# A chunked attention and feed-forward kernel on one core: another order for loads, copies and matmuls

## The chip, the cores and the metric

The kernel runs on one core of one Trainium2 chip. The core has TensorE (PE) for matrix products, VectorE (DVE), ScalarE (ACT) and GpSimd (POOL) for element-wise work, and SyncE (SP), which here only issues transfers. Each engine has a program of its own, and runs it in order. Transfers (DMA) run on 16 DMA engines; here POOL issues the loads (the software queue, q0), and SP the stores and the transpositions from SBUF to SBUF (the hardware queue, q1). The metric is the device time of one execution in microseconds (us); the median of several runs counts.

## What is computed

For 4 batches of 768 tokens and 8 heads of 64, each chunk of 32 queries attends to 8 memory keys and to the keys from 16 before to 8 after the chunk. The result, with heads side by side as rows of 512, goes through a layer norm and a two-layer network, and is added to itself:

```python
for c in range(nc):                      # chunk 32, left 16, right 8
    ...
    k_full = np.concatenate([mem_k, k_ctx], axis=2)
    v_full = np.concatenate([mem_v, v_ctx], axis=2)
    scores = scale * np.matmul(q_c, k_full.transpose(0, 1, 3, 2))
    scores = scores - np.max(scores, axis=-1, keepdims=True)
    a = np.exp(scores)
    a = a / (np.sum(a, axis=-1, keepdims=True) + 1e-09)
    out[:, :, c_start:c_end] = np.matmul(a, v_full)
...
xn = (x - mu) / np.sqrt(var + 1e-06) * g_ln
ch = np.maximum(xn @ w_ch1, 0.0) @ w_ch2      # 512 -> 2048 -> 512
return (x + ch).astype(np.float32)
```

## The kernel before

**Tiles and turns.** 128 tokens are a token tile; a batch has six (t = 0 to 5), the program 24. Three token tiles make a turn u of the network, so there are eight turns (0 to 7), and batch b fills turns 2b and 2b + 1. A turn has U = 28 steps. Steps 0 to 15 are up steps (`up`, line 331: xT times a piece of W1, then a ReLU into rT on ACT or DVE by turns), steps 16 to 27 are down steps (`down`, line 357: rT times W2); after the last one of a tile, `finish` (line 366, DVE) makes the output tile osb and SP stores it. Turn 0 has most of its up steps in the front, the hand-written stretch before the turns; there and in turn 1 some are tile-wise (`up_tile`, line 342: one token tile, four pieces).

**Attention of a token tile.** `scores` (line 244, PE) needs the keys KT and the queries QR of the tile; `soften` (line 254, ACT) takes the exponential; `values` (line 265, PE) needs V, and on DVE it divides and sums (lines 272 to 279); `norm` (line 285, DVE) makes xn; `turn_x` transposes xn into xT, in turns 0 and 1 with PE (line 313) and a copy, later with a DMA transposition on SP (line 308). `stats` (line 290, ACT) and `root` (lines 296 and 300, POOL) give rstd for `finish`. `attend(i, s0, s1, u)` puts these at steps s0 (scores), s0 + 1, s1 (values), s1 + 1 (norm) and s1 + 2 (turn_x, stats) of turn u.

**How K, Q and V come in.** In batch 0 `load_tile` loads K and Q by token tile, and `turn_tile` transposes them with PE (line 194) and copies them to KT and QR. In batches 1 to 3 `load_pair` loads a block of 256 tokens (blk 0, 1, 2), K and Q in two pieces of 128 KB each (line 125); `mix` copies a block into iv with its halves interleaved (line 102, the copy helper); `cross` transposes iv on SP (line 221) into rawk (keys) or QR (queries); `spread` copies rawk to the places in KT where chunks and their neighbours need it (DVE and ACT, lines 102 and 100). `load_v` loads one of twelve V pieces (88 KB, line 133), `v_mem` copies the memory values into V, `mem_cols` the memory keys into KT. There are two sets of KT, QR and V, two rawk, four iv, and eight load buffers st.

**What sets the order.** Nothing is scheduled by a tool: the program is written by hand, and every engine gets its instructions in the order in which the Python emits them. `at(u, step, ...)` puts a call behind the matmuls of a step; `ahead` spreads a list of calls over steps. Where two calls have one step, the one put down first comes first. So a step's number says behind which others a call stands in the queue of its engine, and not when it runs. The loads on POOL wait as well for the one issued eight before.

For batch b > 0 the list `order` (line 596) holds loads, `mem_cols`, `v_mem` and `mix`, all on POOL. Batch 1's list begins at step 23 of turn 0; batches 2 and 3 have theirs in turns 2 and 4. Transpositions and spreads stand in a table of (block, step): for batch 1 `cross` at 27 of turn 0 and at 1 and 14 of turn 1, each spread four steps after that number; for the others `cross` at 7, 12 and 24 and the spread four steps later.

## Time and profile before

| | before |
|---|---|
| median of 3 runs | 265.72 us (264.95 to 266.97) |
| the profiled execution | 263.43 us, its span 261.7 us |
| PE busy | 220.0 us (84%) |
| POOL, DVE, ACT busy | 142.7, 122.3, 97.6 us |
| mean granted clock of PE | 0.908 |
| HBM | 29.82 MB read, 6.29 MB written |

A span reaches from the first to the last instruction of the profiled execution; times in the rows count from its start. In brackets behind a row stands how long the engine had been idle just before, and whose end released it. The lines are those of the kernel before. In this execution turn 0's first down step begins at 43.23 us, turn 1 at 59.58, turn 2 at 103.23, turn 3 at 136.63, turn 4 at 163.21 and turn 5 at 189.29.

### The profile page before, as it was taken

What the parts mean: (1) busy time and instruction counts of PE and PEld (TensorE: products, weight loads), DVE (VectorE), ACT (ScalarE), POOL (GpSimd) and SP (SyncE); (2) the same over time, 40 slices, a digit from 0 to 9 for tenths busy, and PEclk for the clock granted to TensorE, in tenths of its full rate; (3) what the DMA queues carried; (4) which work ended last, traced back from release to release, by engine and by line L of the source; (5) the groups of instructions that cost most, each with busy time, mean ns of one, the idle gap of its engine ahead of it and who ended that gap; (6) DMA issues with size and microseconds to landing.
All of it is one profiled execution on the core that took longest, in us unless ns stands there. A gap on an engine that the chain in (4) does not pass through costs nothing.

```text
span 261.7 us, 5110 instructions
## 1 busy us (share of the span) xinstructions
PE 220.0 (84%) x2048; PEld 132.2 (51%) x2048; DVE 122.3 (47%) x288; ACT 97.6 (37%) x195; POOL 142.7 (55%) x188
## 2 busy tenths in 40 slices
PE   7545988988074998999419999999799999999994
PEld 2324874446053844664105654664366456546653
DVE  5534266475033555570533652582557436443312
ACT  2321255443034461690203740492267216512300
POOL 8936279999817978993494268998301201110000
PEclk9955599999656899999956999999999999999999
DMA  5999999998999998999999937999943230122012
GB/s 78 150 183 196 202 181 130 126 107 131 116 92 129 118 142 133 158 79 90 97 187 98 143 49 124 149 123 129 192 98 23 66 97 10 34 60 80 3 40 80
DMA packets 105448, 28.93 MB, mean 111 GB/s; under 512 B 93392, under 2 KB 101840, under 8 KB 105424
## 3 DMA queue, kind: packets, MB, share of 16 engines
q0 software_dynamic: 72320, 14.84, 65.9%
...
HBM read 29.82 MB, written 6.29 MB: 138 GB/s over the span
## 4 chain that ended last, share of the span: by engine, by line
PE 47%; DMA 26%; POOL 18%; issue 4%; DVE 2%; ACT 2%; POOLq 0%; ACTq 0%; DVEq 0%
DMA st<-in_q_dram 22%; PE mm L331 19%; PE mm L357 18%; POOL V L133 7%; POOL st L125 4%; DMA rawk<-iv 3%; PE mm L342 3%; POOL iv L102 3%; PE att L244 2%; PE att L265 2%; POOL rstd L300 1%; PE mm L379 1%; DMA xT<-xn 1%; POOL V L102 1%; POOL st L117 1%
## 5 line engine op out<-in xcount | busy, mean ns | idle before, releaser
L331 PE MATMUL mm<-xT,w1c 128*128 128x384 f16 (+1 forms) x480 | 86.3, 333 | 12.7 <-DMA xT<-xn 11.7
L357 PE MATMUL mm<-w2c,rT 128*128 128x512 f16 x368 | 83.8, 379 | 0.0
L331 PEld LDWEIGHTS <-w1c 128*128 128x128 f16 x480 | 53.1, 117 | 36.8 <-DMA xT<-xn 10.8
L325 DVE TENSOR_SCALAR rT<-mm 128x384 f16<-128x384 f32 (+2 forms) x65 | 35.6, 549 | 40.7 <-PE mm L331 33.2
L357 PEld LDWEIGHTS <-rT 128*128 128x128 f16 x368 | 34.6, 98 | 38.8
L323 ACT ACTIVATE rT<-mm 128x384 f16<-128x384 f32 (+2 forms) x65 | 31.2, 483 | 59.9 <-PE mm L331 28.1
L133 POOL DMA_DIRECT2D V<-in_v_dram x48 | 44.3, 929 | 1.9 <-DMA st<-in_k_dram 1.0
L296 POOL TENSOR_SCALAR veps<-sq 128x1 f32<-128x1 f32 x24 | 5.9, 248 | 57.0 <-ACT junk L290 34.9
L254 ACT ACTIVATE AT<-att,band 96x512 f16<-96x512 f32 x48 | 31.2, 678 | 7.4 <-PE att L244 7.3
L100 ACT COPY KT<-rawk 128x288 f16<-128x288 f16 (+1 forms) x18 | 12.2, 726 | 45.6 <-DMA rawk<-iv 45.6
L366 DVE SCALAR_TENSOR_TENSOR osb<-mm,rstd,xs 128x512 f32<-128x512 f32 x23 | 17.1, 749 | 24.3 <-PE mm L357 18.6
L102 POOL COPY iv<-st 128x1024 f16<-128x1024 f16 x18 | 19.0, 1074 | 16.4 <-DMA st<-in_q_dram 8.5
L290 ACT ACTIVATE junk<-xs,nmean 128x512 f16<-128x512 f32 x24 | 17.2, 716 | 15.0 <-DVE nmean L279 10.9
L102 DVE COPY KT<-rawk 128x704 f16<-128x704 f16 x9 | 8.4, 936 | 30.6 <-DMA rawk<-iv 30.6
L102 POOL COPY V<-memv 8x2560 f16<-8x2560 f16 x9 | 21.3, 2362 | 0.0
L342 PE MATMUL mm<-xT,w1c 128*128 128x128 f16 x160 | 14.2, 263 | 7.6 <-ACT rT L323 3.8
L285 DVE SCALAR_TENSOR_TENSOR xn<-xs,nmean,gb 128x512 f16<-128x512 f32 x24 | 19.9, 829 | 0.4
L342 PEld LDWEIGHTS <-w1c 128*128 128x128 f16 x160 | 13.4, 129 | 8.4 <-issue 8.0
L273 DVE SCALAR_TENSOR_TENSOR xs<-att,rec 128x512 f32<-128x512 f32 x24 | 16.6, 692 | 0.8
L300 POOL TENSOR_TENSOR rstd<-veps,mhalf 128x1 f32<-128x1 f32 x24 | 13.9, 579 | 2.0
L244 PEld LDWEIGHTS <-KT 64*96 64x96 f16 x384 | 11.4, 129 | 6.8 <-issue 4.5
L244 PE MATMUL att<-QR,KT 64*96 64x64 f16 x384 | 14.2, 216 | 0.6 <-DVE KT L102 0.6
...
## 6 DMA issues: line engine op xcount, KB each, us to landing
...
st<-in_k_dram POOLq DMA_DIRECT2D x24, 128.0 KB, 8.2
st<-in_q_dram POOLq DMA_DIRECT2D x24, 128.0 KB, 9.6
...
```

Source lines behind the costliest of these rows:

```text
L102: eng.tensor_copy(out=out, in_=in_)
L133: nc.gpsimd.dma_start(out=V[b % 2][lo:hi, g, :, 0:64], in_=dram(v, b * H * HS + (64 * g - 24 + lo) * D, [[64, hi - lo], [HS, H], [1, 64]]),)
L244: nc.tensor.matmul(out=p[0:W, par, (4 * gg + j) * 64 : (4 * gg + j) * 64 + 64], lhsT=KT[b % 2][rows, 2 * t + gg, j, :], rhs=free(QR[b % 2] ...
L254: nc.scalar.activation(out=free(AT[t % 3], 32 * c, [[64, 16], [1, 32]]), in_=free(p, 4 * c, [[64, 16], [1, 4], [8, 8]], W), func=ACTF.Exp, ...
L285: nc.vector.scalar_tensor_tensor(out=xn[i % 4], in0=xs[i % 9], scalar=nmean[t], in1=gb, op0=ALU.add, op1=ALU.mult,)
L290: nc.scalar.activation(out=junk, in_=xs[(NT * b + t) % 9], func=ACTF.Square, bias=nmean[t], scale=1.0, accum_out=sq[t],)
L323: nc.scalar.activation(out=o, in_=p, func=ACTF.Relu)
L325: nc.vector.tensor_scalar(out=o, in0=p, scalar1=0.0, scalar2=None, op0=ALU.max)
L331: nc.tensor.matmul(out=p, lhsT=free(w1c[c][:, dt, :], i, [[4, 128]]), rhs=xT[u % 2][:, dt, 128 * lo : 128 * (lo + n)], start=(dt == 0), st ...
L342: nc.tensor.matmul(out=p[:, 128 * k_ : 128 * k_ + 128], lhsT=free(w1c[c][:, dt, :], k_, [[4, 128]]), rhs=xT[u % 2][:, dt, 128 * i : 128 * ...
L357: nc.tensor.matmul(out=p, lhsT=rT[c][:, k_, 128 * i : 128 * i + 128], rhs=w2c[c][:, k_, :], start=(c == 0 and k_ == 0), stop=(c == 3 and k ...
L366: nc.vector.scalar_tensor_tensor(out=o, in0=p, scalar=rstd[t % 9], in1=xs[t % 9], op0=ALU.mult, op1=ALU.add,)
```

## The change

The computation stays as it is. What moves:

- **Front, loads.** The layer-norm weights gb are loaded first of all, from ACT's queue instead of SP's and without the memset ahead. On POOL V pieces 0 and 1 come ahead of query tile 1, and W1 chunk 1 ahead of query tile 2 and key tile 3.
- **Front, PE.** Values and norm of tile 0, its up steps, and tile 1 up to its first up steps come ahead of the transposition of query tile 2 and of key tile 3. W1 chunk 2's up steps move from turn 0 into the front, tile-wise: turn 0 keeps steps 12 to 15. One small key copy goes to ACT. The casts of the memory values of batches 1 to 3 move from the front into turn 0's steps 22 to 24, and batch 1's buffers are cleared at step 15 instead of 12.
- **Batch 1.** The first two blocks are interleaved by ACT (keys) and DVE (queries) at steps 5 and 9 of turn 1, and by POOL only the third; POOL's list keeps the loads and `mem_cols`, and starts at step 21 of turn 0. Transpositions stand at steps 6, 10 and 19, spreads at 12, 15 and 27, scores of tiles 0 to 2 at 13, 16 and 19. `v_mem` goes to DVE.
- **Batches 2 and 3.** Each call has its own step: loads at 0 to 2 and 13, V at 1, 9, 14 to 17 and 21 to 24, `mix` (POOL) at 8, 12 and 20, `cross` at 14, 18 and 26, spreads at 20, 24 and at 4 of the next turn; `v_mem` on DVE at 21, 23, 25.

```diff
-                copy(e0, free(kt, 768 * t - 384 + 88, [[96, 4], [1, 8]]),
+                copy(eo or e0, free(kt, 768 * t - 384 + 88, [[96, 4], [1, 8]]),
...
+    nc.scalar.dma_start(out=gb, in_=dram(moe_g_ln, 0, [[0, 128], [1, 512]]))
     nc.sync.dma_start(out=memkf, in_=dram(mem_k, 0, [[64, 128], [128 * 64, 2], [1, 64]]))
...
-    load_tile(0, 1, 1)
     load_v(0, 0)
     load_v(0, 1)
+    load_tile(0, 1, 1)
     load_tile(0, 2, 0)
     load_w1(0)
     load_v(0, 2)
     load_v(0, 3)
+    load_w1(1)
     load_tile(0, 2, 1)
     load_tile(0, 3, 0)
-    load_w1(1)
...
-    turn_tile(0, 2, 0, dve, act, mm[0])
+    values(0, 0)
+    norm(0, 0)
+    turn_tile(0, 2, 0, dve, act, mm[0], act)
     warm(1)
     scores(0, 1)
     soften(0, 1, 0)
     soften(0, 1, 1)
-    values(0, 0)
-    norm(0, 0)
-    warm(2)
-    turn_tile(0, 2, 1, dve, act, mm[2])
     turn_x(0, 0)
     warm(2)
+    up_tile(0, 0, 0, act)
     values(0, 1)
     norm(0, 1)
+    warm(3)
+    turn_x(0, 1)
+    warm(1)
+    up_tile(0, 0, 1, dve)
+    up_tile(0, 1, 0, act)
+    turn_tile(0, 2, 1, dve, act, mm[2])
     turn_tile(0, 3, 0, dve, act, mm[1])
-    up_tile(0, 0, 0, act)
     scores(0, 2)
...
-    at(0, 9, v_mem, 0, 6, NG, dve)
-    at(0, 12, early, 1)
+    at(0, 14, v_mem, 0, 6, NG, dve)
+    at(0, 15, early, 1)
+    for b in range(1, B):
+        at(0, 14, load_mem_v, b)
+        at(0, 21 + b, mem_vals, b)
...
+            order = [(load_pair, (0,)), (load_pair, (1,)), (mem_cols, (pool,))]
+            order += [(load_v, (g,)) for g in range(6)] + [(load_pair, (2,))]
+            order += [(load_v, (g,)) for g in range(6, 12)]
+            ahead(1, order, 21, 0.25)
+            at(1, 5, mix_pair, 1, 0, act, dve)
+            at(1, 6, cross_pair, 1, 0)
+            at(1, 9, mix_pair, 1, 1, act, dve)
+            at(1, 10, cross_pair, 1, 1)
+            at(1, 12, spread, 1, 0, dve, act)
+            at(1, 15, spread, 1, 1, dve, act)
...
-            ahead(b, order, U * (u - 1), 1)
...
+            at(w, 14, cross_pair, b, 0)
+            at(w, 18, cross_pair, b, 1)
+            at(w, 26, cross_pair, b, 2)
+            at(w, 20, spread, b, 0, dve, act)
+            at(w, 24, spread, b, 1, dve, act)
...
-                    if step >= 8:
+                    if step >= 12:
```

How the instructions stand now, at three places. A minus marks a row of the kernel before, a plus one of the kernel after, and a row without either stands in both; instructions that only wait are not shown.

POOL, the loads of batch 1: V_96 is batch 1's V, iv the interleaved blocks, st the load buffers, memv the memory values, memKT the memory keys.

```order
 L102 COPY KT_98<-memKT 128x48x8
-L102 COPY V_96<-memv_67 8x2560
-L102 COPY iv_89<-st_87 128x2x8x64
-L102 COPY iv_90<-st_88 128x2x8x64
 L133 DMA V_96<-in_v_dram 72x8x64
-L133 DMA V_96<-in_v_dram 88x8x64 x2
-L102 COPY iv_91<-st_81 128x2x8x64
-L102 COPY iv_92<-st_82 128x2x8x64
-L102 COPY V_96<-memv_67 8x2560
-L133 DMA V_96<-in_v_dram 88x8x64 x3
+L133 DMA V_96<-in_v_dram 88x8x64 x5
 L125 DMA st_83<-in_k_dram 128x1x512 x2
```

The copies that stood between the loads are gone from POOL here; behind the first V piece five more follow at once, then the third block.

DVE, turn 1 around the norm of token tile 5 (xn_114<-xs_109): KT_98<-rawk_93 is the spread of batch 1's first block, iv_90<-st_88 the interleaving of its queries, rT a ReLU.

```order
 L273 SCALAR_TENSOR_TENSOR xs_109,tot_131<-att_160,rec_158 128x512
 L279 TENSOR_SCALAR nmean_137<-tot_131 128x1
-L102 COPY KT_98<-rawk_93 128x8x88
-L325 TENSOR_SCALAR rT_120<-mm_161 128x256
+L102 COPY iv_90<-st_88 128x2x8x64
+L325 TENSOR_SCALAR rT_120<-mm_164 128x256
 L285 SCALAR_TENSOR_TENSOR xn_114<-xs_109,nmean_137,gb 128x512
 L318 COPY xT_118<-att_159 128x4x128
```

In the place of the spread, ahead of the norm, stands now a copy that reads loaded data; the spread itself has moved eight rows further back.

SP, turn 2: xT1 is the input of turn 3, one row per token tile, with the last one from xn3_116; the rows into rawk and QR0 are the first two blocks of batch 2.

```order
+L308 DMA_TRANSPOSE xT1_118<-xn1_114 128x4x128
+L308 DMA_TRANSPOSE xT1_118<-xn2_115 128x4x128
 L221 DMA_TRANSPOSE rawk1_94<-iv2_91 128x8x128
 L221 DMA_TRANSPOSE QR0_99<-iv3_92 128x8x128
-L308 DMA_TRANSPOSE xT1_118<-xn1_114 128x4x128
 L221 DMA_TRANSPOSE rawk0_93<-iv0_89 128x8x128
 L221 DMA_TRANSPOSE QR0_99<-iv1_90 128x8x128
-L308 DMA_TRANSPOSE xT1_118<-xn2_115 128x4x128
 L369 DMA out_0_dram<-osb0_123 128x512
 L308 DMA_TRANSPOSE xT1_118<-xn3_116 128x4x128
```

The first two tiles of xT1 now come ahead of all four block transpositions, and the third tile comes directly behind the four and a store.

## Rows read from the trace of the kernel before

**Rows 1.** Busy us by turn: PE, PEld, DVE, ACT, POOL; clock; DMA share; GB/s

```profile
43.23:59.58 16.35, 15.65 (x203) 7.42 (x201) 9.52 (x21) 7.03 (x14) 15.93 (x18) 1.00 0.97 105
59.58:103.23 43.65, 29.98 (x309) 20.77 (x308) 17.95 (x42) 15.47 (x32) 32.88 (x44) 0.80 1.43 126
103.23:127.40 24.17, 24.17 (x208) 13.66 (x208) 9.37 (x21) 10.10 (x21) 16.64 (x16) 1.00 1.51 101
127.40:136.63 9.23, 0.05 (x2) 0.01 (x1) 5.42 (x11) 2.16 (x4) 8.20 (x14) 0.74 1.77 155
136.63:163.21 26.58, 26.48 (x209) 14.65 (x210) 12.03 (x28) 10.87 (x22) 14.69 (x20) 0.90 1.03 107
163.21:187.40 24.19, 24.19 (x209) 13.62 (x207) 14.24 (x30) 12.27 (x24) 21.21 (x24) 1.00 1.54 142
187.40:189.29 1.89, 0.00 (x1) 0.03 (x2) 0.75 (x1) 0.00 (x0) 0.00 (x0) 1.00 1.16 217
```

**Rows 2.** Timeline of PE: start, us, instruction, idle before and its releaser

```profile
19.85 0.63 PE L194 MATMUL mm<-identity,st 64*64 64x64 f16 x16 [3.52 <-DMA st<-in_q_dram]
...
25.45 1.86 PE L342 MATMUL mm<-xT,w1c 128*128 128x128 f16 x16 [2.43 <-ACT KT L100]
...
61.02 1.94 PE L331 MATMUL mm<-xT,w1c 128*128 128x256 f16 x16
...
73.57 0.61 PE L313 MATMUL att<-identity,xn 128*128 128x128 f16 x4 [9.24 <-DVE xn L285]
...
82.26 1.86 PE L342 MATMUL mm<-xT,w1c 128*128 128x128 f16 x16 [3.75 <-ACT rT L323]
...
136.63 4.03 PE L331 MATMUL mm<-xT,w1c 128*128 128x384 f16 x12 [9.18 <-DMA xT<-xn]
```

**Rows 3.** Timeline of DVE, with one row of ACT

```profile
8.38 1.00 DVE L102 COPY V<-memv 8x2560 f16<-8x2560 f16 x1
...
71.72 1.36 ACT L100 COPY KT<-rawk 128x288 f16<-128x288 f16 x2 [8.34 <-DMA rawk<-iv]
71.72 0.81 DVE L102 COPY KT<-rawk 128x704 f16<-128x704 f16 x1 [7.22 <-DMA rawk<-iv]
...
72.77 0.75 DVE L285 SCALAR_TENSOR_TENSOR xn<-xs,nmean,gb 128x512 f16<-128x512 f32 x1
...
127.37 0.81 DVE L102 COPY KT<-rawk 128x704 f16<-128x704 f16 x1 [10.25 <-DMA rawk<-iv]
```

**Rows 4.** Timeline of POOL

```profile
42.58 1.50 POOL L125 DMA_DIRECT2D st<-in_k_dram  x2
...
74.51 1.04 POOL L102 COPY iv<-st 128x1024 f16<-128x1024 f16 x1 [3.53 <-DMA st<-in_k_dram]
79.32 1.04 POOL L102 COPY iv<-st 128x1024 f16<-128x1024 f16 x1 [3.77 <-DMA st<-in_q_dram]
...
85.52 1.44 POOL L125 DMA_DIRECT2D st<-in_k_dram  x2
```

**Rows 5.** Timeline of SP's queue

```profile
61.06 2.84 SPq L221 DMA_TRANSPOSE rawk<-iv  x1
...
131.63 1.24 SPq L308 DMA_TRANSPOSE xT<-xn  x1
```

**Rows 6.** DMA queues (packets, MB, share) in windows 50:53, 72:76, 80:84, 128:132, 188:192

```profile
q0 software_dynamic: 1916, 0.50, 126.1%
...
q1 hardware_dynamic: 773, 0.19, 83.5%
...
q1 hardware_dynamic: 1580, 0.40, 91.9%
...
q0 software_dynamic: 3102, 0.29, 155.3%
...
q1 hardware_dynamic: 2361, 0.92, 102.4%
```

**Rows 7.** Loads of K: transfers, KB each, median us from issue to landing

```profile
st<-in_k_dram POOLq DMA_DIRECT2D x24, 128.0 KB, 8.2
```

More of the change, by code (lines that the diff above doesn't have):

```diff
@@ L395, in warm, with load_mem_v @@
             nc.tensor.matmul(out=p[:, 0:m], lhsT=zero[:, 0:128], rhs=zero[:, 0:m], start=True, stop=True)
+    nc.scalar.dma_start(out=gb, in_=dram(moe_g_ln, 0, [[0, 128], [1, 512]]))
     nc.sync.dma_start(out=memkf, in_=dram(mem_k, 0, [[64, 128], [128 * 64, 2], [1, 64]]))
-    for b in range(B):
+    def load_mem_v(b):
         nc.sync.dma_start(
@@ L402 @@
         )
+    load_mem_v(0)
     PAIR = 1.0 / 128 + 15.0 / 2**20
@@ L514 @@
     soften(0, 2, 1)
-    turn_x(0, 1)
-    up_tile(0, 0, 1, dve)
+    up_tile(0, 1, 1, dve)
     values(0, 2)
     norm(0, 2)
-    up_tile(0, 1, 0, act)
-    up_tile(0, 1, 1, dve)
+    up_tile(0, 2, 0, act)
+    up_tile(0, 2, 1, act)
     turn_x(0, 2)
-    up_tile(0, 0, 2, act)
-    up_tile(0, 1, 2, dve)
+    up_tile(0, 0, 2, dve)
+    up_tile(0, 1, 2, act)
+    up_tile(0, 2, 2, dve)
     for t in range(3):
         stats(0, t)
-    for b in range(1, B):
-        mem_vals(b)
     def early(i):
@@ L588, in load_pair, with mix_pair, cross_pair @@
         load_block(b, blk, 1)
[L590 to L592 removed]
+    def mix_pair(b, blk, e0=pool, e1=pool):
+        mix(b, blk, 0, e0)
+        mix(b, blk, 1, e1)
+    def cross_pair(b, blk):
+        cross(b, blk, 0)
+        cross(b, blk, 1)
     for b in (1, 2, 3):
         u = 2 * b - 1
[L596 to L623 removed]
@@ new lines @@
+        if b == 1:
+            order = [(load_pair, (0,)), (load_pair, (1,)), (mem_cols, (pool,))]
[8 more added lines that the diff above has]
+            at(1, 15, spread, 1, 1, dve, act)
+            at(1, 16, mix_pair, 1, 2)
+            at(1, 19, cross_pair, 1, 2)
+            at(1, 27, spread, 1, 2, dve, act)
+            for i in range(3):
+                at(1, (11, 14, 19)[i], v_mem, 1, 4 * i, 4 * i + 4, dve)
+            attend(6, 13, 16, 1)
+            attend(7, 16, 19, 1)
+            attend(8, 19, 22, 1)
+        else:
+            w = u - 1
+            at(w, 0, load_pair, b, 0)
+            for i in range(2):
+                at(w, 1, load_v, b, i)
+            at(w, 2, load_pair, b, 1)
+            at(w, 8, mix_pair, b, 0)
+            for i in range(2, 4):
+                at(w, 9, load_v, b, i)
+            at(w, 11, mem_cols, b, pool)
+            at(w, 12, mix_pair, b, 1)
+            at(w, 13, load_pair, b, 2)
+            for i in range(4, 8):
+                at(w, 10 + i, load_v, b, i)
+            at(w, 20, mix_pair, b, 2)
+            for i in range(8, 12):
+                at(w, 13 + i, load_v, b, i)
+            at(w, 14, cross_pair, b, 0)
[3 more added lines that the diff above has]
+            at(w, 24, spread, b, 1, dve, act)
+            at(u, 4, spread, b, 2, dve, act)
+            for i in range(3):
+                at(w, (21, 23, 25)[i], v_mem, b, 4 * i, 4 * i + 4, dve)
```

32 lines of the change are left out of this document (1 added, 31 removed).

## The prediction

> **What bounds the kernel now.** I read the busy time by turn first [rows 1], because a share over the whole span hides which turn waits. A turn is 28 steps of TensorE (PE) work on three token tiles. Turn 4 runs without a wait: 24.19 us, PE busy throughout at the full clock. That is the measure for the others. Turn 1 has smaller matmuls, so I build its floor from its pieces: sixteen half-width up steps at 0.485 us (1.94 us for four) [rows 2], four tile-wise up steps at about 1.06, twelve down steps at about 0.86, and some 3.7 us for scores, values and a transposition, 25.8 us in all. It takes 43.65. Turn 3 is preceded by 9.23 us in which PE does next to nothing, and turn 5 by 1.89 [rows 1].
>
> The PE timeline says who ended each wait [rows 2]. In turn 1 it is 9.24 us for VectorE (DVE), then 3.75 us for ScalarE (ACT). DVE itself was not busy: its norm of token tile 5 (line 285) stands in its queue behind the spread of batch 1's keys, which sat until the transposed keys (rawk) had landed at 71.72 [rows 3]. That transposition was issued at 61.06 [rows 5], so it took 10.6 us. Turn 3 has the same pattern: a spread on DVE waited 10.25 us until 127.37, values and norm of the last tile stood behind it, its transposition into xT left SP only at 131.63, and PE started at 136.63 [rows 3, 5, 2]. The granted clock of these stretches is 0.80 in turn 1 and 0.90 in turn 3, against 1.00 elsewhere [rows 1]. PE had been idle before each: the lower of the two levels (1.2 GHz) costs turn 3 26.58 - 24.19 = 2.4 us.
>
> Why a transposition takes 10 us is in the DMA queues [rows 6]. A transposed block is 256 KB and moves as packets of some 256 bytes, about 1,024 of them. In four us, the hardware queue q1 moved 773 packets while K/Q loads were under way, 1,580 beside V loads, and 2,361 (stores among them) nearly alone. I price a block at 5.3, 2.6 and 1.7 us in these three cases.
>
> **The change, part by part.** *Front and turn 0.* PE waits 3.52 us for a query tile and 2.43 us for key copies [rows 2]; now the first up steps stand ahead of that tile, so PE works there, while W1 chunk 1 is loaded ahead of the tile. Four of turn 0's up steps become tile-wise ones in the front: work moved, not removed. Two norm chains of about 2 us on DVE now stand in front of their transpositions, with only 1.3 us of warm-up matmuls over the longer one. Of the 5.95 us I count 2.5 as won. Turn 0 gives back about 1.3: the key copies for its first scores come behind the clearing of batch 1's buffers on DVE (0.8 to 0.9), and the memory-value casts now stand between exponentials on ACT (0.5). Turn 0's 16.35 us of down steps [rows 1] stay otherwise. Turn 1 starts at 58.4 instead of 59.6: **-1.2** (bounds -4 and +1).
>
> *Turn 1.* POOL no longer holds loads behind copies, which is where it waited 3.53 and 3.77 us [rows 4]. The first loads go at 41.3 instead of 42.58 (the roots ahead of them wait for statistics on ACT, done about 1.2 us earlier). K/Q loads move 0.50 MB in 3 us, V loads 0.29 MB in 4 us [rows 6], so a 128 KB piece costs 0.77 us and an 88 KB piece 1.2. From about 46.5, when the front's loads are in: eight K/Q until 53, six V until 60, four K/Q until about 64, six V until 72 or later.
>
> The interleaving copies (mix) wait for nothing then, and cost ACT about 1.1 us each and DVE between 0.4 and 1.1 (the DVE copy of 2,560 elements takes 1.00 [rows 3]; POOL's mix takes 1.04 [rows 4], and shorter runs may cost DVE its speed); I take 0.8. One stands ahead of the norm of tile 5. With a ReLU that costs PE 2.3 us at that transposition, in place of 9.24; it would be 1.2 without the copy. The first keys' transposition goes at 63.4. V loads run beside it by then, perhaps the last K/Q load: at 2.6 to 5.3 us a block the first pair is in by 69.6 to 72.5, the second by 74.8 to 78.6. PE reaches the first scores at 58.4 + 12.4 = 70.8 (4.75 to that transposition, 2.3 of wait, 5.4 of matmuls) and the second 4.8 us after the first (two up steps, two tile-wise ones, a down step, values, scores). I take waits of 0.9 and 1.0 (bounds 0 and 3). The spread (1.36 us on ACT [rows 3]) is inside that. The second scores then start at 77.5, and 11.4 us of PE remain (eleven down steps, two scores, two values): turn 1 ends at 88.9.
>
> *Start of turn 2.* Here the change makes a new wait. POOL mixes batch 1's last block once the first query block is transposed, and then nothing holds it from batch 2's eight K/Q and two V loads, from about 74 instead of 85.52 [rows 4]: 8.6 us of transfers, begun at about 77, behind V. On SP the last two transposed blocks now stand behind a store of turn 1's step 19, so at 81.1, and the last two xT transpositions (half a block each) behind those. The first block at 5.3 us ends at 87, the second at 92 as the loads thin out, the two xT by 95.5. So turn 2 starts at 95.5 instead of 103.23, that is **-6.5** beyond the front's -1.2, and after 6.6 us of idle PE I charge it turn 3's cold start: **+2.4** (bounds for both: no wait, start at 87.2 and warm; start at 103, cold).
>
> *Turn 3.* In turn 2 the spreads stand eight steps later, behind the norm of the last tile, and POOL's loads end by step 12 or so, since only four K/Q pieces and six V are left; the last four V wait for a copy that waits for a transposition. Four blocks go out on SP from 13.6 us into the turn, ahead of the last xT: 4 x 1.7, the store and xT end near 24 to 25 us, against 24.2 of PE. I take 1.0 us of wait for 9.23, and a warm turn: **-8.2 and -2.4** (bounds 0 and 9.2 for the wait).
>
> *Turn 5* has the same order: 0.7 for 1.89, **-1.2**. The memory-value copies move from POOL to DVE, three of about 1 us per batch; DVE has ten us or more of slack in each turn [rows 1], and if one fell between a norm and PE it would cost that 1 us.
>
> The sum is -1.2 - 6.5 + 2.4 - 8.2 - 2.4 - 1.2 = -17.1 us. The profiled execution (span 261.7, whole 263.43) becomes 244.6 and 246.3. The median of the runs shown, 265.72, lies 2.3 above that execution, so I forecast 248.6.
>
> **The rivals.** *Transposes run as if alone* (0.17). Then turn 1 waits only for the norm, turn 2 starts at 87.2 and warm: 248.6 - 8.3 - 2.4 = 237.9. For it: V loads are kinder than K/Q loads, and batch 2's loads might be through before 81. Against it: a K load takes 8.2 us to land in the median [rows 7], and the DMA share is 1.4 to 1.5 in turns 1 and 2. The Trainium skill, "DMA: Bandwidth & Descriptors", section "Anatomy of one DMA", gives about 2.0 us plus bytes over 436 GB/s for a load; by its figure, an estimate, a K/Q piece lands in 2.3 us, and this case would follow. The 8.2 us disagree with it for a queue this full, so the chance stays low.
>
> *The wait of turn 3 stays* (0.13). The last xT now stands behind four blocks on SP instead of two. If the V loads that follow the copy run beside them at 2.6 to 5.3 us a block, the wait is 9.2 us and cold again: 248.6 + 8.2 + 2.4 = 259.2.
>
> *The reordering of turn 1 only moves the wait* (0.11), from norm to scores and to turn 2's start, which stays at 103.2: 248.6 + 7.7 = 256.3. For it: the same bytes share the same transfers, whoever issues them, and they were dense already [rows 1].
>
> *Slower* (0.05): batch 2's earlier loads starve the blocks ahead of xT at the end of turn 1. If q1 got only a third of its 773 packets [rows 6], a block would take some 15 us, the two would end at 111 and turn 2 would start at 114: 248.6 + 18.7 = 267.3. It decides from 95.5 + 17.1 = 112.6 on. Against it: those loads are 8.6 us of transfers and would have to last 30.
>
> **How the numbers follow.** The forecast keeps 0.54, with its own range of 243 to 255 from the bounds of the front and of the two waits of turn 1. The range 237 to 259 takes in the first and third rival, and leaves the second and the slower one outside, under 2 in 10. About 1% is what a measurement of this kernel can tell from no change. All cases but the last lie below 263.1; a mixture of the second and third would come near no change: faster 0.92, same 0.04, slower 0.04.
>
> **What would show it.** In turn 1 the 9.24 us before line 313 should shrink to 2 to 3 us, and the 3.75 us should be gone. A new PE wait for DMA into xT of 4 to 10 us should stand at the start of turn 2, with K/Q loads in flight; if it is missing, the first rival holds. The wait at turn 3's start should be under 3 us, with clock 1.00. The first down step of turn 0 should come near 40.7. If blocks take over 8 us each, or the first scores of batch 1 wait beyond 75, the term of turn 1 is wrong.

## The result, and the profile after

The changed kernel takes 247.64 us in the median (246.49 to 249.02), the kernel before 265.81 (264.95 to 266.97) on the same chip: a ratio of 0.9316 (95% interval 0.9253 to 0.9379). The forecast was 248.6. The profiled execution has a span of 246.4 us where the sum gave 244.6. Here and below, medians are taken over all executions of a run, and ratios only over those within 1.5% of the fastest of their kernel on that chip.

The line of busy time on the changed kernel's page (engine, busy us, share, instructions) shows where it came from: PE is busy for 214.2 us now and was for 220.0, so of the 15.3 us that the span lost, 9.5 are time in which PE stood still and 5.8 are busy time. Its mean granted clock rose from 0.908 to 0.958.

```profile
PE 214.2 (87%) x2082; PEld 129.8 (53%) x2082; DVE 128.5 (52%) x296; ACT 100.2 (41%) x198; POOL 123.5 (50%) x175
```

By turns (start of each in the PE timeline; the predicted column is worked out from the terms of the sum):

| us | before | predicted | after |
|---|---|---|---|
| first down step of turn 0 | 43.23 | 40.7 | 36.52 |
| turn 1 | 59.58 | 58.4 | 54.23 |
| turn 2 | 103.23 | 95.5 | 95.81 |
| turn 3 | 136.63 | 123.1 | 124.22 |
| turn 4 | 163.21 | 147.3 | 148.00 |
| turn 5 | 189.29 | 172.2 | 174.06 |
| end of the span | 261.7 | 244.6 | 246.4 |

The stretches in the changed kernel, with the columns of [rows 1], answer to that group. The first four lines are stretches of the front of the kernel before that stand in no group, the others are the kernel after; some overlap.

```profile
0.00:43.23 43.23, 30.67 (x372) 21.00 (x373) 21.66 (x70) 15.27 (x29) 28.26 (x45) 0.76 1.24 166
12.00:20.00 8.00, 3.66 (x57) 2.13 (x59) 2.46 (x8) 1.69 (x3) 3.77 (x5) 0.52 1.44 183
20.00:43.23 23.23, 18.53 (x222) 15.00 (x221) 11.82 (x31) 9.19 (x19) 13.63 (x22) 0.72 1.37 191
32.00:34.00 2.00, 2.00 (x32) 2.00 (x29) 1.56 (x4) 0.60 (x1) 1.25 (x3) 0.79 1.70 157
...
0.00:36.52 36.52, 28.11 (x406) 19.73 (x407) 18.98 (x59) 13.88 (x27) 24.50 (x38) 0.91 1.26 173
12.00:20.00 8.00, 7.30 (x114) 5.19 (x113) 3.48 (x12) 3.89 (x8) 4.81 (x7) 0.57 1.61 177
18.00:20.00 2.00, 2.00 (x35) 1.75 (x33) 0.09 (x1) 1.04 (x2) 1.04 (x2) 0.76 1.87 164
20.00:36.52 16.52, 13.32 (x220) 11.17 (x219) 8.69 (x21) 7.18 (x16) 8.84 (x13) 1.00 1.28 198
36.52:54.23 17.71, 15.62 (x203) 7.62 (x201) 9.85 (x29) 8.54 (x18) 15.51 (x24) 1.00 1.36 134
54.23:95.81 41.58, 27.18 (x309) 19.35 (x307) 21.22 (x47) 17.72 (x34) 31.45 (x42) 0.90 1.42 151
95.81:124.22 28.41, 26.53 (x208) 14.43 (x209) 16.98 (x33) 12.31 (x24) 13.54 (x15) 0.91 0.96 104
124.22:148.00 23.78, 23.77 (x208) 13.94 (x208) 11.87 (x28) 10.96 (x22) 15.88 (x27) 1.00 1.22 137
148.00:174.06 26.06, 24.19 (x209) 13.65 (x208) 18.19 (x34) 12.26 (x24) 15.62 (x17) 1.00 1.16 134
```

The front is 6.7 us shorter. From 20 us on its clock is 1.00 instead of 0.72, but 20 us is not the same place in the two programs: between 12 and 20 us the changed kernel does 114 matmuls and the kernel before 57. In both, the clock falls to its lower level shortly after 12 us; it is back at the upper one at about 19 us in the changed kernel and at about 33 in the kernel before. Over the whole front, from 0 to the first down step, PE's busy time falls from 30.67 to 28.11 us and its idle time from 12.56 to 8.41.

Turn 1 and the idle time behind it last 41.58 us instead of 43.65. PE's idle time in it rises from 13.67 to 14.40 us; its busy time falls from 29.98 to 27.18, at a clock of 0.90 instead of 0.80. Turn 2 runs at 0.91, turns 3 and 4 at 1.00.

The PE timeline of the changed kernel has these waits from turn 1 on (all others are under 0.6 us):

```profile
60.58 0.40 PE L313 MATMUL att<-identity,xn 128*128 128x128 f16 x4 [1.61 <-DVE xn L285]
...
70.34 0.85 PE L244 MATMUL att<-QR,KT 64*96 64x64 f16 x16 [4.96 <-DMA QR<-iv]
...
95.81 2.75 PE L331 MATMUL mm<-xT,w1c 128*128 128x384 f16 x8 [7.83 <-DMA xT<-xn]
...
124.22 2.11 PE L331 MATMUL mm<-xT,w1c 128*128 128x384 f16 x12 [1.88 <-DMA xT<-xn]
...
174.06 2.14 PE L331 MATMUL mm<-xT,w1c 128*128 128x384 f16 x12 [1.87 <-DMA xT<-xn]
```

Against [rows 2]: the 9.24 us for VectorE are 1.61, the 3.75 for ScalarE are gone, and the 9.18 at turn 3 are 1.88. Two waits are new: 4.96 us for the first queries of batch 1, and 7.83 for xT at the start of turn 2. In turn 1 and up to turn 2 PE waited 9.24 + 3.75 = 12.99 us before, and waits 1.61 + 4.96 + 7.83 = 14.40 now. The wait has moved and not shrunk. Still turn 2 starts 7.4 us earlier: turn 1 starts 5.35 us earlier, and it is 2.07 us shorter, because its busy time is. That says where the time went, and not yet what caused it; for that the runs below are needed.

The first of batch 2's loads in the POOL timeline, two rows of the SP queue (start, time on the queue) and, for these two transfers, the rows that give us from issue to landing:

```profile
71.43 1.44 POOL L125 DMA_DIRECT2D st<-in_k_dram  x2
...
81.03 2.79 SPq L221 DMA_TRANSPOSE rawk<-iv  x1
83.91 6.02 SPq L221 DMA_TRANSPOSE QR<-iv  x1
...
rawk<-iv SPq DMA_TRANSPOSE x1, 10.4
QR<-iv SPq DMA_TRANSPOSE x1, 9.8
```

Batch 2's loads left from 71.43 on (85.52 before [rows 4]), so the two last blocks of batch 1 run among them and land at 91.4 and 93.7; the two xT transpositions stand behind them.

### The profile page after: what moved, and what is told of

Read it like the earlier page. It is cut to its first block, busy times and chain, and to the rows that moved or that the text cites. A ratio compares the mean times of both kernels' runs of the same rounds, so it can differ in the third digit from the quotient of the medians.

```text
span 246.4 us, 5177 instructions
## 1 busy us (share of the span) xinstructions
PE 214.2 (87%) x2082; PEld 129.8 (53%) x2082; DVE 128.5 (52%) x296; ACT 100.2 (41%) x198; POOL 123.5 (50%) x175
## 4 chain that ended last, share of the span: by engine, by line
PE 66%; DMA 16%; DVE 12%; ACT 2%; issue 2%; DVEq 0%; ACTq 0%
PE mm L331 30%; PE mm L357 22%; DMA xT<-xn 6%; DMA rawk<-iv 4%; PE att L244 4%; DMA QR<-iv 4%; PE att L265 4%; PE mm L342 4%; DVE xn L285 2%; DVE xs L273 2%; DMA memkf<-in_mem_k_dram 2%; DVE KT L102 2%; DVE V L102 2%; PE mm L379 1%; ACT AT L254 1%
## 5 line engine op out<-in xcount | busy, mean ns | idle before, releaser
L331 PE MATMUL mm<-xT,w1c 128*128 128x384 f16 (+1 forms) x464 | 80.8, 327 | 11.6 <-DMA xT<-xn 11.6
L331 PEld LDWEIGHTS <-w1c 128*128 128x128 f16 x464 | 50.5, 115 | 33.3 <-DMA xT<-xn 10.7
L133 POOL DMA_DIRECT2D V<-in_v_dram x48 | 49.0, 1025 | 5.4 <-DMA st<-in_k_dram 3.7
L102 POOL COPY iv<-st 128x1024 f16<-128x1024 f16 x14 | 15.6, 1128 | 28.5 <-DMA rawk<-iv 25.3
L244 PEld LDWEIGHTS <-KT 64*96 64x96 f16 x384 | 11.9, 129 | 14.7 <-issue 10.9
L285 DVE SCALAR_TENSOR_TENSOR xn<-xs,nmean,gb 128x512 f16<-128x512 f32 x24 | 18.9, 787 | 0.4
L272 DVE RECIPROCAL rec<-att 128x8 f32<-128x8 f32 x24 | 4.9, 204 | 23.9 <-PE att L265 22.4
L342 PEld LDWEIGHTS <-w1c 128*128 128x128 f16 x208 | 13.8, 118 | 2.0 <-issue 1.8
L265 PEld LDWEIGHTS <-AT 96*64 96x64 f16 x384 | 8.1, 112 | 9.7 <-issue 4.0
## 6 DMA issues: line engine op xcount, KB each, us to landing
w2c<-in_moe_w_ch_dram POOLq DMA_DIRECT2D x4, 512.0 KB, 10.6
```

What stands on the lines that cost most here:

```text
L102: eng.tensor_copy(out=out, in_=in_)
L133: nc.gpsimd.dma_start(out=V[b % 2][lo:hi, g, :, 0:64], in_=dram(v, b * H * HS + (64 * g - 24 + lo) * D, [[64, hi - lo], [HS, H], [1, 64]]),)
L244: nc.tensor.matmul(out=p[0:W, par, (4 * gg + j) * 64 : (4 * gg + j) * 64 + 64], lhsT=KT[b % 2][rows, 2 * t + gg, j, :], rhs=free(QR[b % 2] ...
L265: nc.tensor.matmul(out=p[64 * gg : 64 * gg + 64, par, 128 * j : 128 * j + HD], lhsT=AT[t % 3][:, par, gg, j, :], rhs=V[b % 2][:, 2 * t + g ...
L285: nc.vector.scalar_tensor_tensor(out=xn[i % 4], in0=xs[i % 9], scalar=nmean[t], in1=gb, op0=ALU.add, op1=ALU.mult,)
L331: nc.tensor.matmul(out=p, lhsT=free(w1c[c][:, dt, :], i, [[4, 128]]), rhs=xT[u % 2][:, dt, 128 * lo : 128 * (lo + n)], start=(dt == 0), st ...
```

## The experiments

Each ratio is against runs of the kernel before on the same chip. The starts of turns are those of the profiled execution, which need not be the median one; its time has a column.

| run | median us | ratio to before | 95% interval | profiled us | turn 2, turn 3 start |
|---|---|---|---|---|---|
| changed kernel | 247.64 | 0.9316 | 0.9253 to 0.9379 | 248.19 | 95.81, 124.22 |
| front of before | 246.49 | 0.9195 | 0.9055 to 0.9335 | 247.69 | 97.65, 124.74 |
| batches 2, 3 of before | 255.67 | 0.9613 | 0.9513 to 0.9713 | 255.84 | 93.08, 126.02 |
| batch 1 of before | 254.46 | 0.9508 | 0.9359 to 0.9657 | 253.73 | 104.33, 131.66 |
| loads behind roots | 253.29 | 0.9508 | 0.9386 to 0.9630 | 249.87 | 90.33, 125.53 |
| blocks early | 245.73 | 0.9304 | 0.9263 to 0.9346 | 245.70 | 95.76, 122.81 |
| blocks before xT | 244.52 | 0.9239 | 0.9180 to 0.9298 | 247.78 | 92.68, 122.09 |
| loads late, blocks early | 250.50 | 0.9448 | 0.9371 to 0.9524 | 251.56 | 93.05, 126.32 |
| copies on GpSimd | 248.20 | 0.9400 | 0.9330 to 0.9469 | 251.23 | 96.96, 126.09 |
| both moves | 242.61 | 0.9094 | 0.9018 to 0.9171 | 242.60 | 93.30, 120.01 |
| copies, blocks earlier | 246.56 | 0.9154 | 0.8999 to 0.9310 | 246.38 | 95.17, 123.52 |
| front alone | 267.26 | none | | 267.52 | 101.93, 130.81 |
| changed kernel again | 249.96 | 0.9286 | 0.9184 to 0.9389 | 246.93 | 96.41, 123.78 |

### What the front is worth

The front (lines 398 to 532 of the changed kernel, with turn 0's first plan entries) is put back, the batch loops stay:

```diff
-    nc.scalar.dma_start(out=gb, in_=dram(moe_g_ln, 0, [[0, 128], [1, 512]]))
...
+    load_tile(0, 1, 1)
     load_v(0, 0)
     load_v(0, 1)
-    load_tile(0, 1, 1)
...
-    load_w1(1)
     load_tile(0, 2, 1)
     load_tile(0, 3, 0)
+    load_w1(1)
...
+    nc.sync.dma_start(out=gb, in_=dram(moe_g_ln, 0, [[0, 128], [1, 512]]))
...
```

> The front and turn 0 stand as in the kernel before (its loads, its TensorE order, its load of gb, its places for memory values); batches 1, 2 and 3 stand as in the changed kernel. The traces of the two kernels show the first down step of turn 0 at 36.52 us against 43.23 and the start of turn 1 at 54.23 against 59.58. Theory A, the front is worth what it gains: nothing behind it takes the 5.35 us back, so this kernel takes 247.6 + 5.4 = 253.0 us, and turn 2 starts near 101. Theory B, what follows waits for batch 1's loads, which were issued only 2.3 us earlier (40.29 against 42.58): TensorE, coming later, waits less for the transposed blocks (4.96 and 7.83 us of wait in the changed kernel), turn 2 starts near 98 and the time is about 249.9. My own step in the prediction (the front is worth 1.2 us) would give 248.8.

Measured: 246.49 us (242.40 to 248.71), no slower than the changed kernel, where every theory expected at least 248.8. The PE timeline of that run, and the rows of the last two blocks (us from issue to landing):

```profile
74.26 0.85 PE L244 MATMUL att<-QR,KT 64*96 64x64 f16 x16 [4.99 <-DMA QR<-iv]
97.65 2.75 PE L331 MATMUL mm<-xT,w1c 128*128 128x384 f16 x8 [4.73 <-DMA xT<-xn]
...
rawk<-iv SPq DMA_TRANSPOSE x1, 7.8
QR<-iv SPq DMA_TRANSPOSE x1, 7.0
```

Turn 1 starts at 58.11, 3.9 us later than in the changed kernel, and the first scores of batch 1 are still 3.9 later (74.26 against 70.34). Then the lead shrinks: the last two blocks left at 85.97 and 87.68 and took 7.8 and 7.0 us, not 10.4 and 9.8, PE waits 4.73 instead of 7.83, and turn 2 is 1.84 us later, turn 3 0.5. The lead of the front is given back as a longer wait for the same transfers. One pair of executions would not show that, because landing times spread: in a second execution of the changed kernel these two blocks took 7.8 and 6.4 us. But the waits before the first scores and before turn 2 add up to 12.4 to 12.8 us in three executions of this order behind the new front (the changed kernel, the same again, and blocks early), and to 9.72 here.

The other way round, the front alone on the kernel before. Against the changed kernel, `mix_pair` and the whole loop over b = 1, 2, 3 are those of before:

```diff
...
-            ahead(1, order, 21, 0.25)
...
+            ahead(1, order, 23, 0.3)
...
+            ahead(b, order, U * (u - 1), 1)
...
```

> The kernel before with the front and turn 0 of the changed kernel, and batches 1, 2 and 3 placed as before. The other way round (the changed kernel with the front of before) cost nothing. Theory A, the front gains its 5 us only where nothing behind it waits; in the kernel before, turn 1 waits for transposed keys whose loads leave only 2 us earlier, so nothing or little of it reaches the end: 263.5 to 266 us. Theory B, the front's 5.35 us reach the end here: 260 to 261.5 us.

Measured: 267.26 us (258.91 to 268.47) against 268.98 (261.93 to 274.14) for the kernel before; the executions lie too far apart for an interval, and for a choice between the theories: the medians differ by 1.7 us, the lowest by 3.0. Two waits of the profiled execution, in the PE timeline:

```profile
101.93 2.75 PE L331 MATMUL mm<-xT,w1c 128*128 128x384 f16 x8 [7.55 <-DMA xT<-xn]
...
143.09 4.00 PE L331 MATMUL mm<-xT,w1c 128*128 128x384 f16 x12 [8.23 <-ACT rT L323]
```

Turn 1 starts at 54.60 instead of 59.58, turn 2 only 1.3 us earlier than before (101.93 against 103.23). The wait that stood ahead of turn 3 comes inside it, 8.23 us for a ReLU that is queued behind a spread. That is how Theory A has it, in one execution.

### What the order of batch 1 is worth

```diff
...
-            ahead(1, order, 21, 0.25)
-            at(1, 5, mix_pair, 1, 0, act, dve)
...
+            ahead(1, order, 23, 0.3)
...
+                        at(0, 27, cross, 1, 0, which)
+                at(1, s + 4, spread, 1, blk, dve, act)
...
```

> Batch 1 is placed as in the kernel before (interleaving on GpSimd between the loads, spreads at steps 5, 8 and 18 of turn 1); front, batch 2 and batch 3 as in the changed kernel. Theory A, the order of batch 1 is worth what my prediction gave it: the wait for VectorE in turn 1 returns, turn 1 is some 43.6 us long against 41.6 or, by the prediction's step, 5 us longer: 249.7 to 252.9 us. Theory B, the order of batch 1 only moves the wait from turn 1 to the start of turn 2: 247.6, with 9 us of wait before line 313 and under 4 at the start of turn 2.

`mix_pair` and `v_mem` stand on POOL in the list again, spreads at steps 5, 8 and 18. Measured: 254.46 us (250.55 to 255.59), some 7 more than the changed kernel and a little beyond Theory A; the interval of the ratio begins at 0.9359, where that of the changed kernel ends at 0.9379. Theory B falls: the wait for VectorE is back, and the one at turn 2 stays. The PE timeline:

```profile
69.11 0.61 PE L313 MATMUL att<-identity,xn 128*128 128x128 f16 x4 [6.62 <-DVE xn L285]
78.37 1.87 PE L342 MATMUL mm<-xT,w1c 128*128 128x128 f16 x16 [3.75 <-ACT rT L323]
...
104.33 2.75 PE L331 MATMUL mm<-xT,w1c 128*128 128x384 f16 x8 [6.89 <-DMA xT<-xn]
```

With the runs of the front and that of batches 2 and 3 (below), six of the eight combinations are on record:

| front | batch 1 | batches 2, 3 | turn 2 starts |
|---|---|---|---|
| old | old | old | 103.23 |
| new | old | old | 101.93 |
| new | old | new | 104.33 |
| new | new | old | 93.08 |
| old | new | new | 97.65 |
| new | new | new | 95.81 |

Where only batch 1 differs, its new order is worth 8.9 us (101.93 to 93.08) and 8.5 (104.33 to 95.81). The new steps of batches 2 and 3 cost 2.4 and 2.7 us here, and the new front gives 1.3 and 1.8. These are single executions, and in those of the new front the first down step alone lies anywhere between 36.06 and 38.36 us. So what the front gives at turn 2 is not clear of the spread; what batch 1's order gives is.

Which part of it counts, the engine of the copies or the places? The copies go back to GpSimd, at the same steps:

```diff
-            at(1, 5, mix_pair, 1, 0, act, dve)
+            at(1, 5, mix_pair, 1, 0)
             at(1, 6, cross_pair, 1, 0)
-            at(1, 9, mix_pair, 1, 1, act, dve)
+            at(1, 9, mix_pair, 1, 1)
```

> The changed kernel, with the interleaving copies of batch 1's first two pairs of blocks on GpSimd again (as in the kernel before) at the same steps of turn 1, instead of ScalarE and VectorE. Theory A, the gain of batch 1's new order is the place of loads and spreads, not the engine: the copies wait on GpSimd behind the last loads (about 2 us each pair), the first block leaves 1 to 3 us later, 247.6 to 250 us. Theory B, GpSimd's queue was the bound: the copies stand behind V loads and a VectorE copy until 65 us, the first transposed keys land near 75 instead of 67, turn 1 waits 5 us and more again for VectorE, 253 to 255 us, as with batch 1's old order (254.5).

Measured: 248.20 us, which by the ratio can't be told from the changed kernel; so Theory A has it, but not for its reason: the first block left 7 us later, not 1 to 3. SP's queue, the block's landing time, and PE:

```profile
65.95 1.34 SPq L221 DMA_TRANSPOSE rawk<-iv  x1
rawk<-iv SPq DMA_TRANSPOSE x1, 3.3
...
70.71 0.85 PE L244 MATMUL att<-QR,KT 64*96 64x64 f16 x16 [6.00 <-ACT KT L100]
```

It left at 65.95 instead of 58.99 and landed after 3.3 us instead of 8.0, at 69.3 instead of 67.0; PE reached its scores 0.4 us later. The engine of the copies matters little here: the block that leaves 7 us earlier lands only 2.3 us earlier. Which of the moved places makes the gain (loads, spreads or scores) is not shown.

### What the later steps of batches 2 and 3 are worth

```diff
...
-            at(w, 14, cross_pair, b, 0)
...
-            at(w, 20, spread, b, 0, dve, act)
...
+            ahead(b, order, U * (u - 1), 1)
+            for blk, s in ((0, 7), (1, 12), (2, 24)):
+                at(u - 1, s, cross, b, blk, 0)
...
```

> Batches 2 and 3 are placed as in the kernel before (steps of loads, copies, transpositions, spreads and memory values); front and batch 1 as in the changed kernel. Theory A, the steps of batches 2 and 3 took turn 3's wait away: the wait of 9.2 us for xT at the start of turn 3 comes back, with 2.4 us for the lower clock after it: 247.6 + 7.3 + 2.4 = 257.3 us. Theory B, the wait of turn 3 was inherited from turn 1 (batch 2's loads went late, at 85.52 us of the trace, because batch 1 was late): with batch 1 repaired the old steps do nearly as well, wait under 3 us, 247 to 250 us.

Measured: 255.67 us, 1.6 below Theory A's 257.3, and far from B's. The PE timeline:

```profile
93.08 1.49 PE L331 MATMUL mm<-xT,w1c 128*128 128x384 f16 x8 [1.68 <-DMA xT<-xn]
...
126.02 3.46 PE L331 MATMUL mm<-xT,w1c 128*128 128x384 f16 x12 [7.67 <-DMA xT<-xn]
...
180.20 3.65 PE L331 MATMUL mm<-xT,w1c 128*128 128x384 f16 x12 [3.29 <-DMA xT<-xn]
```

The wait of turn 3 is back (7.67 us, then matmuls at the lower clock: 3.46 for twelve against 2.11), and turn 5's is 3.29. But turn 2 starts 2.7 us earlier than in the changed kernel: the last two blocks of batch 1 left 1.3 to 2.8 us later (83.84 and 85.22) and took 5.7 and 5.3 us. The steps of batch 2 in the change pay for turn 3 with part of turn 2. Which of these steps takes the wait of turn 3 away is not shown.

### Do batch 2's loads delay the blocks at the end of turn 1?

```diff
-        at(i // 3, 12 if i == 5 else 3 + i % 3, root, b, t)
+        at(i // 3, 12 if i == 5 else 0 if 6 <= i < 9 else 3 + i % 3, root, b, t)
```

> The changed kernel, with the three small root computations of turn 1's tokens on GpSimd (steps 3 to 5 of turn 2) emitted at step 0 of turn 2, ahead of batch 2's loads. They wait for statistics that ScalarE finishes at 77 to 86 us, so the eight K/Q loads and two V loads of batch 2 go out near 87 us instead of 71 to 80. Theory A, those loads slow the last two transposed blocks and the xT transpositions behind them: the block issued at 81.0 lands in 4 to 6 us instead of 10.4, the next likewise, xT leaves by 88, turn 2 starts near 91 instead of 95.8 and the time is 242 to 244 us. Theory B, the blocks are slow for their own reasons (V loads still in flight, or the transpositions themselves): turn 2 starts at 95 to 96 as now, and batch 2 comes later, 247 to 250 us.

Measured: 253.29 us. At the place in question Theory A is right within a microsecond, and the time still goes the other way. The landing times of the two blocks, and the PE timeline:

```profile
rawk<-iv SPq DMA_TRANSPOSE x1, 3.9
QR<-iv SPq DMA_TRANSPOSE x1, 3.2
...
90.33 2.55 PE L331 MATMUL mm<-xT,w1c 128*128 128x384 f16 x8 [2.30 <-DMA xT<-xn]
...
125.53 3.38 PE L331 MATMUL mm<-xT,w1c 128*128 128x384 f16 x12 [9.44 <-DMA xT<-xn]
```

The block issued at 81.08 takes 3.9 us instead of 10.4, the next 3.2 instead of 9.8, and turn 2 starts at 90.33. In three executions with the loads in their place these blocks took 6.4 to 10.4 us. This shows the cause of the 7.83 us: loads in flight. But the loads that leave at 87 fill turn 2 instead: its first two blocks, issued at 106.47 and 109.92, take 11.9 us each, not 3.2 and 3.3, the last xT leaves at 122.28 instead of 118.71, and the wait at turn 3 grows from 1.88 to 9.44.

Is it the place of those blocks? Both edits together:

```diff
-        at(i // 3, 12 if i == 5 else 3 + i % 3, root, b, t)
+        at(i // 3, 12 if i == 5 else 0 if 6 <= i < 9 else 3 + i % 3, root, b, t)
...
-            at(w, 14, cross_pair, b, 0)
-            at(w, 18, cross_pair, b, 1)
+            at(w, 9, cross_pair, b, 0)
+            at(w, 12, cross_pair, b, 1)
```

> Both edits in one: batch 2's loads behind the root computations of turn 1 on GpSimd, so out near 87 us instead of 71 to 80, and the first two pairs of transposed blocks of batches 2 and 3 at steps 9 and 12. With the first edit alone turn 2 started at 90.33 us after a wait of 2.30, but the wait at turn 3 grew to 9.44, with the last pair of blocks and the last V loads late behind 112 us. Theory A, that wait came from the place of the blocks behind the second xT (106.5 us): now they leave from about 99 to 103, the wait at turn 3 falls under 3 us, turn 3 starts near 119 and the time is 240 to 243 us. Theory B, the wait came from the number of transfers that are left for turn 2, wherever the blocks stand: it stays over 6 us, 248 to 252 us.

Measured: 250.50 us, Theory B. The timelines of POOL and PE:

```profile
115.59 1.04 POOL L102 COPY iv<-st 128x1024 f16<-128x1024 f16 x1 [4.41 <-DMA st<-in_k_dram]
...
126.32 4.03 PE L331 MATMUL mm<-xT,w1c 128*128 128x384 f16 x12 [7.52 <-DMA xT<-xn]
```

The third pair's loads, issued at 104.84, kept its copy waiting until 115.59, so the last V loads left at 121 beside the last xT. With the loads this late, the place of the blocks does not help.

### Two moves that help, and one that does not

The four blocks of batches 2 and 3 ahead of the turn's second xT:

```diff
-            at(w, 14, cross_pair, b, 0)
-            at(w, 18, cross_pair, b, 1)
+            at(w, 9, cross_pair, b, 0)
+            at(w, 12, cross_pair, b, 1)
```

> The changed kernel, with the first two pairs of transposed blocks of batches 2 and 3 at steps 9 and 12 of turns 2 and 4 instead of 14 and 18, so that on SyncE they stand ahead of the second xT transposition of the turn, which waits for its norm until 112 us of the trace. Their copies were done by 95 us, so they can leave at 107 instead of 112.2; the last V loads, which wait on GpSimd for these blocks, follow 5 us earlier, and the last xT leaves alone. Theory A, the four blocks are what holds the last xT: the waits of 1.88 and 1.87 us at the starts of turns 3 and 5 fall under 0.5, the time is 244 to 245.5 us. Theory B, the last xT waits for its norm and takes its 5 us whatever stands before it: waits of 1.5 to 2 stay, 247.6 us.

Measured: 245.73 us (244.87 to 246.01); by the ratio it can't be told from the changed kernel. The trace shows the waits of 1.88 and 1.87 us at 0.58 and 0.78, nearly Theory A; in a second execution of the changed kernel they are 1.72 and 1.08. The PE timeline:

```profile
122.81 2.14 PE L331 MATMUL mm<-xT,w1c 128*128 128x384 f16 x12 [0.58 <-DMA xT<-xn]
...
171.58 2.14 PE L331 MATMUL mm<-xT,w1c 128*128 128x384 f16 x12 [0.78 <-DMA xT<-xn]
```

The last blocks of batch 1 ahead of the first xT of turn 1:

```diff
-            at(1, 19, cross_pair, 1, 2)
+            at(1, 17, cross_pair, 1, 2)
```

> The changed kernel, with the last pair of transposed blocks of batch 1 at step 17 of turn 1 instead of 19: on SyncE ahead of the xT transposition of token tile 6, which waits for its norm until 78.4 us, instead of behind it and a store. The copies for it were done by 71.5, so the blocks leave near 72 and 75 instead of 81 and 84, beside the last V loads and batch 2's K/Q loads. Theory A, what makes turn 2 late is that xT stands behind two blocks: the blocks land by 86 to 88 in any case, the two last xT leave at 83 and 87 and turn 2 starts near 92: 243 to 245 us. Theory B, the transfers in flight set the end: blocks take 12 us or more, tile 6's xT now stands behind them too, turn 2 starts at 95 to 97 as now: 247 to 249 us.

Measured: 244.52 us (242.96 to 247.78), in the range of Theory A, though by the ratio alone this can't be told from the changed kernel either. The blocks left at 70.14 and 72.31, the last two xT at 84.30 and 88.05 instead of 89.99 and 91.96. PE at the start of turn 2:

```profile
92.68 2.33 PE L331 MATMUL mm<-xT,w1c 128*128 128x384 f16 x8 [3.46 <-DMA xT<-xn]
```

Not all of it is kept in this execution: turn 3 starts after a wait of 3.66 us.

Both together:

```diff
-            at(1, 19, cross_pair, 1, 2)
+            at(1, 17, cross_pair, 1, 2)
...
-            at(w, 14, cross_pair, b, 0)
-            at(w, 18, cross_pair, b, 1)
+            at(w, 9, cross_pair, b, 0)
+            at(w, 12, cross_pair, b, 1)
```

> The two moves that gained, in one kernel: the last pair of blocks of batch 1 at step 17 of turn 1, the first two pairs of batches 2 and 3 at steps 9 and 12 of turns 2 and 4. Theory A, they take away different waits (at the start of turn 2, and at the starts of turns 3 and 5): 3.1 and 1.9 us add, 242 to 243 us, with under 4 us of wait at turn 2 and under 1 at turns 3 and 5. Theory B, an earlier turn 2 leaves turn 3's transfers less time, and what the first move gains comes back as wait at turn 3: 244 to 246 us.

Measured: 242.61 us, ratio 0.9094 (0.9018 to 0.9171). On the same chip the changed kernel took 249.96, ratio 0.9286 (0.9184 to 0.9389). The intervals don't meet, so this version beats both kernels, the changed one by some 2%; Theory A. The PE timeline:

```profile
93.30 2.55 PE L331 MATMUL mm<-xT,w1c 128*128 128x384 f16 x8 [3.98 <-DMA xT<-xn]
...
120.01 2.14 PE L331 MATMUL mm<-xT,w1c 128*128 128x384 f16 x12 [0.96 <-DMA xT<-xn]
...
168.49 2.14 PE L331 MATMUL mm<-xT,w1c 128*128 128x384 f16 x12 [0.48 <-DMA xT<-xn]
```

The three waits for xT are 3.98, 0.96 and 0.48 us, against 7.83, 1.88 and 1.87, and 6.75, 1.72 and 1.08 in a second execution of the changed kernel. That is the last run here, the changed kernel with no edit:

> The changed kernel itself, on the chip of these runs, as a measure for the two kernels above: 246.5 to 248.5 us, and 243 to 246 of it are not expected from any theory.

The median of that run, 249.96, lies above the expected range: three executions took 246.93 to 248.76 us and three 251.16 to 252.89. The ratio, 0.9286, agrees with the first one, 0.9316.

The remaining wait of 5 us in turn 1, attacked by an earlier departure:

```diff
-            at(1, 5, mix_pair, 1, 0, act, dve)
-            at(1, 6, cross_pair, 1, 0)
...
+            at(1, 0, mix_pair, 1, 0, act, dve)
+            at(1, 1, cross_pair, 1, 0)
...
```

The second pair's calls move from 9 and 10 to 4 and 5, the third pair's transposition to 16, and both moves stand in it too.

> The kernel with both moves, and in turn 1 the interleaving copies and transposed blocks of batch 1's first two pairs at steps 0, 1, 4 and 5 instead of 5, 6, 9 and 10 (their loads had landed by 53 us), and the third pair's blocks at step 16. The spreads stay where they are. Theory A, the wait of about 5 us before the first scores of batch 1 is the time of two blocks, and they now leave 2.5 to 3 us earlier: that wait falls to 2 to 3, turn 2 starts 2 us earlier too: 239.5 to 241 us. Theory B, the V loads in flight until 72 us set when the blocks land, not when they leave: the wait stays near 5, and copies ahead of ReLUs cost up to 1 us: 242 to 244 us.

Measured: 246.56 us (242.61 to 247.59), above either theory by the median; by the ratio, 0.9154 against 0.9094, it can't be told from both moves. For the wait itself Theory B is nearer. SP's queue, the block's landing time, and PE:

```profile
55.58 1.78 SPq L221 DMA_TRANSPOSE rawk<-iv  x1
rawk<-iv SPq DMA_TRANSPOSE x1, 10.6
...
69.53 0.55 PE L244 MATMUL att<-QR,KT 64*96 64x64 f16 x16 [4.38 <-DMA QR<-iv]
...
95.17 2.75 PE L331 MATMUL mm<-xT,w1c 128*128 128x384 f16 x8 [7.75 <-DMA xT<-xn]
```

The block left 3.4 us earlier than in the changed kernel and landed 0.8 earlier (66.2 against 67.0); the wait fell from 4.96 to 4.38. Why the wait at turn 2 is 7.75 in this execution is open: the three xT left some 2 us earlier than with both moves, and the first two landed earlier as well (85.8 and 91.8 against 91.5 and 92.2), but the last only near 95, beside K loads of batch 2 of which one took 17 us.

## Why the prediction was right, and where it was not

**Total.** 248.6 against 247.64, and 244.6 against 246.4 in the trace. The closer total has some luck in it: I added 2.3 us for the median over the profiled execution, and the profiled execution of the changed kernel (248.19 in all) lies 0.5 above its median. Two smaller sums of the prediction are off: the floor of turn 1 adds up to 26.0, not 25.8, and the slower rival's 18.7 should be 18.5. Nothing else rests on them.

**Front: wrong in place, right in worth.** The step said that the first down step would come at 40.7 and turn 1 start at 58.4; they came at 36.52 and 54.23. Two terms were mis-sized. I counted 2.5 us of waiting as won, and PE's idle time fell by 4.15. And I left the busy time of the front as it was; it fell by 2.56 us although 406 matmuls stand there instead of 372, with the clock back at its upper level some 14 us earlier. Yet the 1.2 us that I gave the front is near what the runs show at turn 2 (1.3 and 1.8, not clear of the spread), and at the end they show none. That was not my reasoning: I had argued that little is won, and the runs show that much is won and given back in waits for transposed blocks. Turn 0 gave back 17.71 - 16.35 = 1.36 us, as the 1.3 of the step, and in its places: PE waits 1.24 us for copies behind the clearing of batch 1's buffers and 0.51 us for an exponential.

**Turn 1: the waits.** Norm: 2.3 predicted, 1.61 measured; about half of the difference is VectorE's copy, 0.43 and 0.51 us where I had taken 0.8. First scores: 0.9 predicted with a bound of 3, 4.96 measured; this is the step that failed. The landing came as predicted: the pair was to be in by 69.6 to 72.5 (two blocks at the step's own prices, from 63.4 on, give 68.6 to 74.0), and it was in at 70.3. But PE stood there at 65.38, not at 70.8, and the block, which with the earlier turn left at 58.99 and not at 63.4, hardly landed earlier for it: the pair took 11.3 us, 5.7 each, where I had priced a block at 2.6 to 5.3. The transposing queue of the changed kernel in the windows 58:62 and 62:66 (packets, MB, share):

```profile
q1 hardware_dynamic: 164, 0.28, 19.8%
...
q1 hardware_dynamic: 1181, 0.29, 58.2%
```

While K/Q loads were in flight, q1 moved 164 packets in 4 us, stores among them, and not the 773 of the price; behind them, beside V loads, 1,181. The 773 were one window of the kernel before; another of its windows with K/Q loads, 116:120, has 354. Two runs with other departures agree that no price per block holds here: the first block left at 55.58, 58.99 or 65.95 and landed at 66.2, 67.0 or 69.3. Second scores: 1.0 predicted, none measured. PE's turn 1 ended at 87.98 (88.9 predicted).

**Start of turn 2: right, with some luck.** 7.83 us of wait for 6.6, start at 95.81 for 95.5, and batch 2's loads as the cause, which the loads behind roots show by taking the blocks from 10.4 to 3.9 us. That the start agrees to 0.3 us has luck in it: turn 1 began 4.2 us too early and waited 4.1 us too long. The first block was to land at 87 and the second at 92; they took 10.4 and 9.8 us and landed at 91.4 and 93.7. So the prediction's own sign of a wrong price (blocks over 8 us each) came. The 6.5 us beyond the front, for the new orders together, measure 5.6 with the old front (103.23 to 97.65) and 6.1 with the new (101.93 to 95.81): batch 1 gives 8.5 to 8.9, and batch 2's earlier loads and later steps take 2.4 to 2.7 back. The cold start was 26.53 - 24.17 = 2.36 us against [rows 1], 2.4 predicted.

**Turn 3: right.** 1.88 us of wait for 1.0, and turn 3 warm at 23.78. The four blocks left 16.4 us into turn 2 (13.6 predicted). Putting batches 2 and 3 back gives 7.67 us and the lower clock again.

**Turn 5: little or nothing.** 1.87 us against 1.89 before, where I had 0.7; the second execution of the changed kernel has 1.08. The blocks left 14.1 us into turn 4 (13.6 predicted) and the last xT 21.2 into it, at 169.18. It took 4.8 us to land, beside the V loads that POOL sent once its copies were free, so it landed at 26.0 where I had 24 to 25: the mis-sized term is that xT. With the blocks ahead of the second xT the wait falls to 0.78.

**The rivals.** That transposed blocks run as if alone: with the loads held back they do (3.2 to 3.9 us), at the end of turn 1 of the changed kernel they don't (10.4 and 9.8). K loads land in 6.7 us in the median here, 8.2 before [rows 7]. The fit of the Trainium skill, "DMA: Bandwidth & Descriptors", "Anatomy of one DMA", on which that rival leaned, gives 2.3, an estimate; the trace disagrees in both kernels. The Trainium skill, "Advanced Engine Details and Errata", section "X-Bar Transpose (TRN2)", holds transposing transfers to be about as fast as others, 350 to 400 GB/s, which would be 0.7 us for a block, an estimate; no run here comes near it: the quickest block took 3.1 us from issue to landing, and where four followed each other with no load beside them (112 to 116 us of the changed kernel) q1 moved 0.64 MB in 4 us, 160 GB/s. That turn 1 only moves the wait: true of the waits added up (12.99 and 14.40 us), false of the time, since the order of batch 1 is worth 8.5 us and more at turn 2. That batch 2's loads starve the blocks: they do, by 6.5 us a block, not enough to reach the 112.6 from which it would have been slower.
